# Two decoder layers on one core: gate and up weights resident, keys in two buffers, the first LayerNorm transposed on TensorE

## The chip, the cores and the metric

The kernel runs on one core of one Trainium2 chip. The metric is device time in microseconds (us) of one execution. Engines: PE is TensorE's matmul, PEld its weight load, DVE is VectorE, ACT is ScalarE, POOL is GpSimd, SP is SyncE, which issues all the transfers here.

## What is computed

Two layers, each a sliding-window attention block and a gated feed-forward block with residuals, over 2048 tokens of width 512 (bf16). Both layers use the same weights.

```python
def _A_ref(x, wqkv, wo):                 # H = 32 heads of 16, window W = 256
    qkv = (x @ wqkv).reshape(B, S, 3, H, Dh).transpose(2, 0, 3, 1, 4)
    q, k, v = qkv[0], qkv[1], qkv[2]
    scores = jnp.einsum("bhqd,bhkd->bhqk", q, k) * (Dh ** -0.5)
    mask = (idx[:, None] - idx[None, :] >= 0) & (idx[:, None] - idx[None, :] < W)
    scores = jnp.where(mask[None, None], scores, -1e9)
    o = jnp.einsum("bhqk,bhkd->bhqd", softmax(scores), v)
    return o.transpose(0, 2, 1, 3).reshape(B, S, D) @ wo

def _B_ref(x, w_gate, w_up, w_down):     # F = 1792
    h = sigmoid(x @ w_gate) * (x @ w_up)
    return h @ w_down

x = A_x
x = x + _A_ref(layernorm(x), A_wqkv, A_wo)
x = x + _B_ref(layernorm(x), B_w_gate, B_w_up, B_w_down)
x = x + _A_ref(layernorm(x), A_wqkv, A_wo)
x = x + _B_ref(layernorm(x), B_w_gate, B_w_up, B_w_down)
```

## The kernel before

The 2048 tokens are 16 tiles of 128, in four groups of 512. A group of a layer has the number gi = 4 * layer + group. The residual stream x stays in SBUF (`xsb`).

**Slots.** `run` (L459) writes the order of all instructions out by hand. It walks 256 slots: 16 tiles a layer, eight slots a tile, four heads a slot. A slot issues the scores of four heads (L337) into four fixed PSUM banks (`Sps`) and the exponential of them (L341) into a ring. Every second slot multiplies the diagonal block of eight heads by a triangular mask (L348) and, on POOL, cuts the far block (L353). Six slots after its scores, half a tile's values are summed (L366), copied (L371), transposed on PE a slot later (L383), normalized (L391, L393), transposed back by a DMA (L397), and two slots after that the output projection (L419) adds to x (L421).

**Streams.** The projections and the feed-forward parts are streams of units, put between: a projection stream has 12 units of four 512-column matmuls (keys and queries of four column groups, L224, and values of four tiles, L240). A GLU stream has 14 gate units (L284, then a tanh on ACT, L287), 14 up units (L295, then a multiply on DVE, L297), and three down units per tile (L307, then an add into x, L310); the half-group streams have 256 columns a unit in place of 512. After the last slot the streams that are left run alone: the tail. The list `order` (L464) ranks the streams; `next_stream` (L446) takes the first that has units, whose LayerNorm tiles are ready and whose `free_slot` has come, and never a second GLU stream before the first is done. Units are popped as long as the planner's nanoseconds leave room:

```python
if st_ is None or used + st_.units[0][0] // 2 > T_SLOT:
    break
```

`used` has 370 ns for scores, 868 for values, 228 for the transposes, 864 for an output projection. `ensure` (L433) pops what a slot needs and what isn't done yet. Keys, queries and values of a group go to buffers kTp[gi % 3] and Vaug[gi % 3]; `gi_free_slot` (L429) lets a projection stream start only when its buffers are free: slot 0 for gi 0 to 2, then 58, 90, 122, 154 and 186.

**LayerNorm.** `ln_stats` (L147) on DVE and a power on POOL, `ln_apply` (L158) on DVE one slot later, `ln_move` (L166) transposes a tile by a DMA from SP into `xnT`, which has three buffers of a group each; a tile counts as ready LN_LAG = 2 slots later. A LayerNorm whose group finds no free xnT buffer is put off slot by slot (L188). Groups 1 to 3 of layer 0 follow in slots 0 to 10.

**Weights.** wqkv, wo and w_down stay in SBUF. Gate and up weights are loaded again in each GLU stream, in seven chunks of 256 columns, through three buffers (`load_chunk`, L267), each chunk by two DMAs that the gate unit issues on SP's queue (L278), where the transposes are issued too, in order.

Of the kernel before, what the change touches and what calls it, by code (L numbers as in the profile page):

```python
# [11 lines left out]
P = 128  # L12
# [20 lines left out]
T_SLOT = 2000  # L33
# [27 lines left out]
class Net:  # L61
# [3 lines left out]
    def __init__(self, ctx, tc, A_x, wqkv, wo, w_gate, w_up, w_down, out):  # L65
# [15 lines left out]
        self.wgup = pool("wgu", 3)  # L81
# [17 lines left out]
        self.maskq = big.tile([P, 8, P], BF16, name="maskq")  # L99
# [30 lines left out]
        self.chunk_w = {}  # L130
        self.chunk_next = 0
        self.states = {}

    def constants(self):
        nc = self.nc
        for i in range(3):
            ones = self.Vaug[i][:, :, 0:VS * H].rearrange("p t (h c) -> p t h c", c=VS)[:, :, :, 16:VS]
            nc.gpsimd.memset(ones, 1.0)
            nc.gpsimd.memset(self.Vaug[i][:, :, VS * H:VW], 0.0)
            if i == 0:  # L140
                nc.gpsimd.memset(self.maskq[:], 1.0)
                nc.gpsimd.affine_select(out=self.maskq[:], in_=self.maskq[:], compare_op=ALU.is_ge, fill=0.0,
                                        base=0, pattern=[[0, 8], [1, P]], channel_multiplier=-1)
# [57 lines left out]
    def proj_stream(self, L, tg):  # L201
        key = ("p", L, tg)
        gi = L * NTG + tg
        b = gi % 3
        s = Stream(key, self.gi_free_slot(gi))
        tiles = range(tg * NBG, (tg + 1) * NBG)
        s.needs = [(key, t) for t in tiles]
        for cq in range(NCQ):
            for which in (1, 0):
                s.add(KT * T_MM, ("kq"[which == 0], gi, cq), lambda which=which, cq=cq: self._qk(key, tg, b, which, cq))  # L210
        for tt in range(NBG):
            s.add(KT * T_MM, ("v", gi, tt), lambda tt=tt: self._v(key, tg, b, tt))
        if gi == 0:
            v0 = s.units.pop(8)
            s.units.insert(4, v0)
        return s

    def _qk(self, key, tg, b, which, cq):
# [3 lines left out]
        c0 = which * D + cq * P  # L222
# [24 lines left out]
    def glu_stream(self, L, t0, n):
# [19 lines left out]
    def load_chunk(self):  # L267
        i = self.chunk_next
        self.chunk_next += 1
        f0 = (i % (FC // 2)) * 2 * P  # L270
        w = self.wgup.tile([P, KT, 2, 2 * P], BF16, name="wgu")
        self.nc.sync.dma_start(out=w[:, :, 0, :], in_=self.wg_src[:, :, f0:f0 + 2 * P])
        self.nc.sync.dma_start(out=w[:, :, 1, :], in_=self.wu_src[:, :, f0:f0 + 2 * P])
        self.chunk_w[i] = w

    def _gate(self, key, i, fc, c0, w):
# [41 lines left out]
    def scores(self, L, t, g):  # L318
# [13 lines left out]
        kTp = self.kTp[(L * NTG + t // NBG) % 3]  # L332
# [126 lines left out]
    def run(self):  # L459
        nc = self.nc  # L460
        self.slot = 0
        self.chunks = 0
        self.streams = []
        order = [("p", 0, 0), ("p", 0, 1), ("p", 0, 2), ("p", 0, 3), ("g", 0, 0, 2), ("g", 0, 2, 2), ("p", 1, 0),  # L464
                 ("g", 0, 4, 4), ("p", 1, 1), ("g", 0, 8, 4), ("p", 1, 2), ("g", 0, 12, 4), ("p", 1, 3),
                 ("g", 1, 0, 4), ("g", 1, 4, 4), ("g", 1, 8, 4), ("g", 1, 12, 2), ("g", 1, 14, 2)]
        for o in order:
            self.streams.append(self.proj_stream(*o[1:]) if o[0] == "p" else self.glu_stream(*o[1:]))
        k0 = ("p", 0, 0)
        for t in range(NBG):  # L470
# [13 lines left out]
        for t in range(NBG, 2 * NBG):  # L484
            self.at((t - NBG) // 2, 0, lambda t=t: self._ln_rest(("p", 0, 1), t))
        for t in range(2 * NBG, NT):
            self.at(t - 6, 0, lambda t=t: self.ln_later(("p", 0, t // NBG), t))
        self.at(12, 0, lambda: nc.vector.tensor_scalar(out=self.wd[:], in0=self.wd[:], scalar1=0.5, scalar2=None,
# [90 lines left out]
```

## Time and profile before

| | us |
|---|---|
| median of three runs | 680.45 |
| the fastest of them | 676.07 |
| the profiled execution | 677.35 |
| its span, first to last instruction | 675.6 |

The profiled execution is 1.75 us longer than its span. In the views, "busy" of PE counts matmuls that overlap in its pipeline. A figure after "<-" in brackets is idle time of that engine just before the instruction, and what ended it. PEclk is the clock granted to TensorE, as a share of full speed.

### The profile page before, as it was taken

To read this page: it belongs to the slowest core of one execution; us is meant where nothing else is said; L and a number is where in the kernel's file an instruction comes from. 1 tells how busy PE (TensorE), PEld (TensorE's weight loads), DVE (VectorE), ACT (ScalarE), POOL (GpSimd) and SP (SyncE) were. 2 spreads that over 40 slices of the span, in tenths; PEclk is the share of its full clock that TensorE was granted. 3 is DMA by queue.
4 is the path that set the end of the run, shared out by engine and by line. 5 is a ranking of instruction groups with operands and counts; after the bars stand their busy time and mean duration, and the time that the engine had idled before them with its cause. 6 is when DMAs were issued, how large, how long until landed. Compare 5 with 4: busy or idle time off the path is not lost.

```text
span 675.6 us, 17143 instructions
## 1 busy us (share of the span) xinstructions
PE 592.3 (88%) x7200; PEld 282.1 (42%) x7200; DVE 422.9 (63%) x851; ACT 459.1 (68%) x493; POOL 164.9 (24%) x191
## 2 busy tenths in 40 slices
PE   0689688686969999899998999999999998999697
PEld 0234354453423444444433444444444443445454
DVE  5497556658544656867588766866556656666322
ACT  0599666566876878766767897688868876752211
POOL 3352222223221222420023223322222222200000
PEclk9899899789868999999999999999999998999889
DMA  9621353352002420254113511243114522442553
GB/s 249 177 53 25 87 153 87 83 137 63 18 9 80 118 71 14 44 108 125 40 33 62 140 49 49 57 125 79 49 47 80 142 63 59 111 111 72 147 158 89
DMA packets 135629, 58.53 MB, mean 87 GB/s; under 512 B 55936, under 2 KB 135552, under 8 KB 135552
## 3 DMA queue, kind: packets, MB, share of 16 engines
q1 hardware_dynamic: 135552, 57.44, 33.4%
q8 instruction: 56, 0.92, 0.6%
q14 instruction: 21, 0.17, 0.1%
HBM read 42.73 MB, written 2.10 MB: 66 GB/s over the span
## 4 chain that ended last, share of the span: by engine, by line
PE 64%; ACT 12%; DVE 10%; DMA 9%; issue 2%; SPq 1%; POOL 1%; ACTq 0%; POOLq 0%; DVEq 0%
PE ups L295 14%; PE gps L284 13%; PE dps L307 10%; ACT PTring L341 9%; PE Sps L337 8%; PE proj_ps L224 7%; PE OTps L366 6%; PE OPps L419 3%; DMA wgu<-in_B_w_up_dram 3%; PE tps L383 2%; DVE xn L162 2%; DMA wgu<-in_B_w_gate_dram 2%; DVE ln_stats L152 2%; DVE PTring L348 2%; DMA xnT<-xn 2%
## 5 line engine op out<-in xcount | busy, mean ns | idle before, releaser
L341 ACT ACTIVATE PTring<-Sps 128x1536 bf16<-128x1536 f32 (+2 forms) x256 | 351.9, 1375 | 94.2 <-PE Sps L337 87.3
L353 POOL TENSOR_SCALAR_AFFINE_SELECT PTring<-PTring 128x1024 bf16<-128x1024 bf16 x112 | 124.4, 1113 | 182.5 <-ACT PTring L341 182.5
L284 PE MATMUL gps<-xnT,wgu 128*128 128x512 bf16 (+1 forms) x560 | 126.4, 351 | 20.7 <-DMA wgu<-in_B_w_gate_dram 14.9
L297 DVE SCALAR_TENSOR_TENSOR hT<-gth,ups 128x512 bf16<-128x512 bf16 (+1 forms) x140 | 81.0, 579 | 94.1 <-PE ups L295 71.5
L295 PE MATMUL ups<-xnT,wgu 128*128 128x512 bf16 (+1 forms) x560 | 126.5, 351 | 5.1 <-DMA wgu<-in_B_w_up_dram 1.7
L287 ACT ACTIVATE gth<-gps 128x512 bf16<-128x512 f32 (+1 forms) x140 | 71.3, 512 | 81.1 <-PE gps L284 76.2
L337 PE MATMUL Sps<-qT,kTp 32*128 32x128 bf16 (+2 forms) x1984 | 87.6, 248 | 25.6 <-ACT PTring L341 21.3
L155 POOL TENSOR_TENSOR ln_rs<-ln_rs,nhalf 128x1 f32<-128x1 f32 x64 | 38.3, 599 | 288.5 <-DVE ln_rs L154 283.6
L307 PE MATMUL dps<-wd,hT 128*128 128x512 bf16 x448 | 107.4, 380 | 0.0
L348 DVE TENSOR_TENSOR PTring<-PTring,maskq 128x1024 bf16<-128x1024 bf16 x128 | 98.8, 772 | 0.3 <-ACT PTring L341 0.2
L337 PEld LDWEIGHTS <-kTp 32*128 32x128 bf16 x1984 | 38.5, 93 | 128.5 <-issue 122.7
L224 PE MATMUL proj_ps<-xnT,wq 128*128 128x512 bf16 x256 | 66.9, 398 | 18.2 <-DMA xnT<-xn 17.2
L284 PEld LDWEIGHTS <-wgu 128*128 128x128 bf16 x560 | 51.9, 101 | 64.3 <-DMA wgu<-in_B_w_gate_dram 17.9
L295 PEld LDWEIGHTS <-wgu 128*128 128x128 bf16 x560 | 52.7, 102 | 49.1 <-issue 8.3
L371 DVE CAST OTs<-OTps 128x512 bf16<-128x512 f32 x64 | 44.1, 688 | 45.8 <-PE OTps L366 44.8
L307 PEld LDWEIGHTS <-hT 128*128 128x128 bf16 x448 | 40.3, 98 | 45.0 <-issue 2.5
L366 PE MATMUL OTps<-PTring,Vaug 128*32 128x128 bf16 x2880 | 53.2, 223 | 0.0
L162 DVE TENSOR_SCALAR xn<-xsb,ln_mv,ln_rs 128x512 bf16<-128x512 bf16 x64 | 47.5, 749 | 4.6 <-POOL ln_rs L155 3.8
L152 DVE BATCH_NORM_STATS2 ln_stats<-xsb 128x6 f32<-128x512 bf16 x64 | 44.3, 692 | 6.4 <-DMA xsb<-in_A_x_dram 4.8
L366 PEld LDWEIGHTS <-Vaug 128*32 128x32 bf16 x2880 | 41.8, 98 | 9.1 <-issue 5.7
L224 PEld LDWEIGHTS <-wq 128*128 128x128 bf16 x256 | 23.2, 101 | 44.9 <-DMA xnT<-xn 17.2
L310 DVE TENSOR_TENSOR xsb<-xsb,dps 128x512 bf16<-128x512 bf16 x32 | 21.9, 683 | 31.7 <-PE dps L307 31.4
(31 smaller groups left out, 304.4 us busy)
## 6 DMA issues: line engine op xcount, KB each, us to landing
wgu<-in_B_w_gate_dram SPq DMA_DIRECT2D x70, 256.0 KB, 3.2
wgu<-in_B_w_up_dram SPq DMA_DIRECT2D x70, 256.0 KB, 3.8
out_dram<-xsb SPq DMA_DIRECT2D x16, 128.0 KB, 1.7
wd<-in_B_w_down_dram SPq DMA_DIRECT2D x1, 1792.0 KB, 9.4
wq<-in_A_wqkv_dram SPq DMA_DIRECT2D x3, 512.0 KB, 6.0
xsb<-in_A_x_dram SPq DMA_DIRECT2D x3, 512.0 KB, 8.9
xnT<-xn SPq DMA_TRANSPOSE x64, 2.4
OnT<-On SPq DMA_TRANSPOSE x64, 2.3
```

The source lines that it names most:

```text
L162: nc.vector.tensor_scalar(out=xn[:], in0=self.xsb[:, t, :], scalar1=mv[:, 0:1], scalar2=rs[:, 1:2], op0=ALU.subtract, op1=ALU.mult)
L224: nc.tensor.matmul(pt[:], lhsT=self.wq[:, kt, c0:c0 + P], rhs=xnT[:, kt, :], start=(kt == 0), stop=(kt == KT - 1))
L284: nc.tensor.matmul(ps[:, 0:w], lhsT=wt[:, kt, 0, (fc % 2) * P:(fc % 2 + 1) * P], rhs=xnT[:, kt, c0:c0 + w], start=(kt == 0), stop=(kt == K ...
L287: nc.scalar.activation(out=self.th[:, 0:w], in_=ps[:, 0:w], func=AF.Tanh, scale=0.5)
L295: nc.tensor.matmul(ps[:, 0:w], lhsT=wt[:, kt, 1, (fc % 2) * P:(fc % 2 + 1) * P], rhs=xnT[:, kt, c0:c0 + w], start=(kt == 0), stop=(kt == K ...
L297: nc.vector.scalar_tensor_tensor(out=self.hT[:, fc, 0:w], in0=self.th[:, 0:w], scalar=1.0, in1=ps[:, 0:w], op0=ALU.add, op1=ALU.mult)
L307: nc.tensor.matmul(self.dps[:], lhsT=self.hT[:, fc, tt * P:(tt + 1) * P], rhs=self.wd[:, fc, :], start=(fc == 0), stop=(fc == FC - 1))
L337: nc.tensor.matmul(sps[:, m, i * P:(i + n) * P], lhsT=kTp[32 * m:32 * m + 32, cq, e, ko:ko + P], rhs=self.qT[32 * m:32 * m + 32, cq, (t + ...
L341: nc.scalar.activation(out=self.ring[:, h0:h0 + 7:2, p0:p0 + (nb - 1) * step + 1:step, :], in_=sps[:, :, 0:N].rearrange("p w (b c) -> p w ...
L348: nc.vector.tensor_tensor(out=r0, in0=r0, in1=self.maskq[:], op=ALU.mult)
L353: self.nc.gpsimd.affine_select(out=r2, in_=r2, compare_op=ALU.is_ge, fill=0.0, base=-1, pattern=[[0, 8], [-1, P]], channel_multiplier=1)
L366: nc.tensor.matmul(OT[32 * g:32 * g + 32, col, :], lhsT=Va[:, jj % NBG, VS * h:VS * h + 32], rhs=self.ring[:, h, ring_slot(jj, t - jj), :] ...
```

## The change

Gate and up weights get SBUF tiles of their own (`wg`, `wu`), loaded once; `load_chunk`, its pool and its 140 loads go. Room comes from kTp (two buffers in place of three), the mask (one 128-column block, read eight times, in place of eight blocks) and one xn buffer less. With two key buffers, keys of group gi may be made only from slot 32 (gi - 1) on, so the keys of later groups are streams of their own; values keep their three buffers and dates. A group's xnT is freed when all its units, the late keys too, are done. The four first tiles are transposed on PE and copied by ACT, and count as ready at once. Tiles 4 to 7 take their LayerNorm statistics in the slots in place of ahead of them. wo, then gate and up in quarters of 448 columns in turn, then w_down in two halves are issued on SP in slots 3, 5, ..., 23; the halving of w_down on DVE moves from slot 12 to 26. T_SLOT goes from 2000 to 1900.

```diff
-T_SLOT = 2000
+T_SLOT = 1900
...
-        self.ln_xn = pool("ln_xn", 4)
+        self.ln_xn = pool("ln_xn", 3)
...
+        self.wg = big.tile([P, KT, F], BF16, name="wg")
+        self.wu = big.tile([P, KT, F], BF16, name="wu")
...
-        self.kTp = [big.tile([P, NCQ, 2, TGW], BF16, name=f"kTp{i}") for i in range(3)]
+        self.kTp = [big.tile([P, NCQ, 2, TGW], BF16, name=f"kTp{i}") for i in range(2)]
...
-        self.maskq = big.tile([P, 8, P], BF16, name="maskq")
+        self.maskq = big.tile([P, 1, P], BF16, name="maskq")
...
-    def ln_move(self, key, t):
+    def ln_move(self, key, t, pe=False):
...
-        if LN_DMA:
+        if LN_DMA and not pe:
             nc.sync.dma_start_transpose(out=dst, in_=xn[:])
         else:
             pt = self.ps_d.tile([P, KT, P], BF16, name="ln_tp", tag="d")
             for c in range(KT):
                 nc.tensor.transpose(pt[:, c, :], xn[:, c * P:(c + 1) * P], self.ident[:])
-            nc.vector.tensor_copy(out=dst, in_=pt[:])
-        self.ready[key, t] = self.slot + (LN_LAG if LN_DMA else 1)
+            nc.scalar.copy(out=dst, in_=pt[:])
+        self.ready[key, t] = self.slot + (0 if pe else LN_LAG if LN_DMA else 1)
...
-    def proj_stream(self, L, tg):
+    def proj_stream(self, kinds, L, tg):
...
+        free = 0
+        if "k" in kinds and gi >= 2:
+            free = TGW // P * SLOTS_T * (gi - 1)
+        if "v" in kinds and gi >= 3:
+            free = max(free, (4 * (gi - 3) + 6) * SLOTS_T + 10)
+        s = Stream(key, free)
...
-        while self.chunk_next < min(i + 3 - (fc % 2 == 0), self.chunks):
-            self.load_chunk()
-        wt = self.chunk_w[i]
...
-            nc.tensor.matmul(ps[:, 0:w], lhsT=wt[:, kt, 0, (fc % 2) * P:(fc % 2 + 1) * P], rhs=xnT[:, kt, c0:c0 + w], start=(kt == 0),
+            nc.tensor.matmul(ps[:, 0:w], lhsT=self.wg[:, kt, fc * P:(fc + 1) * P], rhs=xnT[:, kt, c0:c0 + w], start=(kt == 0),
...
-        nc.vector.tensor_tensor(out=r0, in0=r0, in1=self.maskq[:], op=ALU.mult)
+        nc.vector.tensor_tensor(out=r0, in0=r0, in1=self.maskq[:].to_broadcast([P, 8, P]), op=ALU.mult)
...
-        order = [("p", 0, 0), ("p", 0, 1), ("p", 0, 2), ("p", 0, 3), ("g", 0, 0, 2), ("g", 0, 2, 2), ("p", 1, 0),
-                 ("g", 0, 4, 4), ("p", 1, 1), ("g", 0, 8, 4), ("p", 1, 2), ("g", 0, 12, 4), ("p", 1, 3),
+        order = [("kqv", 0, 0), ("kqv", 0, 1), ("qv", 0, 2), ("qv", 0, 3), ("g", 0, 0, 2), ("k", 0, 2), ("g", 0, 2, 2),
+                 ("qv", 1, 0), ("k", 0, 3), ("k", 1, 0), ("g", 0, 4, 4), ("qv", 1, 1), ("k", 1, 1), ("g", 0, 8, 4),
+                 ("qv", 1, 2), ("k", 1, 2), ("g", 0, 12, 4), ("qv", 1, 3), ("k", 1, 3),
                  ("g", 1, 0, 4), ("g", 1, 4, 4), ("g", 1, 8, 4), ("g", 1, 12, 2), ("g", 1, 14, 2)]
...
-        for t in range(NBG, 2 * NBG):
-            self.ln_stats(("p", 0, 1), t)
         self.constants()
-        nc.sync.dma_start(out=self.wot[:], in_=self.wo_src)
-        nc.sync.dma_start(out=self.wd[:], in_=self.wd_src)
...
+        loads = [load(self.wot[:], self.wo_src)]
+        for i in range(4):
+            h = slice(i * F // 4, (i + 1) * F // 4)
+            loads += [load(self.wg[:, :, h], self.wg_src[:, :, h]), load(self.wu[:, :, h], self.wu_src[:, :, h])]
+        loads += [load(self.wd[:, i * 7:i * 7 + 7, :], self.wd_src[:, i * 7:i * 7 + 7, :]) for i in range(2)]
+        for i, fn in enumerate(loads):
+            self.at(3 + 2 * i, 0, fn)
+        self.at(26, 0, lambda: nc.vector.tensor_scalar(out=self.wd[:], in0=self.wd[:], scalar1=0.5, scalar2=None,
```

## Rows read from the trace of the kernel before

**Rows 1.** Page, busy us (share of the span) and instructions of an engine:

```profile
PE 592.3 (88%) x7200; PEld 282.1 (42%) x7200; DVE 422.9 (63%) x851; ACT 459.1 (68%) x493; POOL 164.9 (24%) x191
```

**Rows 2.** Stages: us, busy us (instructions) by engine, PEclk, DMA share, GB/s:

```profile
17.20:77.50 60.30, 50.03 (x516) 21.54 (x516) 42.48 (x98) 51.99 (x60) 22.00 (x30) 0.97 0.31 72
77.50:205.00 127.50, 97.00 (x1362) 53.71 (x1363) 74.29 (x147) 85.55 (x89) 33.41 (x35) 0.85 0.33 85
...
336.00:617.00 281.00, 270.33 (x3414) 120.49 (x3413) 189.77 (x359) 211.94 (x208) 74.66 (x80) 0.99 0.31 77
617.00:675.60 58.60, 48.14 (x357) 30.60 (x354) 20.49 (x46) 11.22 (x29) 0.55 (x1) 0.94 0.46 129
```

**Rows 3.** PE's waits from 77 to 160 us: total us, times, longest:

```profile
PE gps L284 <- DMA wgu<-in_B_w_gate_dram: 8.6, 3, 4.4
PE gps L284 <- DMA xnT<-xn: 2.9, 1, 2.9
```

**Rows 4.** PE's waits from 617 to 676 us, the tail:

```profile
PE gps L284 <- DMA wgu<-in_B_w_gate_dram: 5.9, 3, 2.6
PE ups L295 <- DMA wgu<-in_B_w_up_dram: 1.0, 4, 0.3
```

**Rows 5.** Timeline of the start: start us, us, engine, line, operation [idle before]:

```profile
8.08 7.04 SPq L174 DMA_TRANSPOSE xnT<-xn  x4
8.43 0.41 DVE L162 TENSOR_SCALAR xn<-xsb,ln_mv,ln_rs 128x512 bf16<-128x512 bf16 x1 [0.44 <-POOL ln_rs L155]
...
17.23 3.57 PE L224 MATMUL proj_ps<-xnT,wq 128*128 128x512 bf16 x8 [17.23 <-DMA xnT<-xn]
...
19.13 0.59 ACT L230 CAST kt<-proj_ps 128x512 bf16<-128x512 f32 x1 [17.05 <-PE proj_ps L224]
```

**Rows 6.** Timeline, the exponentials of slots 0, 1 and 2:

```profile
21.86 1.45 ACT L341 ACTIVATE PTring<-Sps 128x1536 bf16<-128x1536 f32 x1 [0.44 <-PE Sps L337]
...
23.76 1.45 ACT L341 ACTIVATE PTring<-Sps 128x1536 bf16<-128x1536 f32 x1 [0.44 <-PE Sps L337]
...
27.88 1.45 ACT L341 ACTIVATE PTring<-Sps 128x1536 bf16<-128x1536 f32 x1 [0.45 <-PE Sps L337]
```

**Rows 7.** Timeline at slot 24, where the first gates begin:

```profile
76.13 1.19 SPq L174 DMA_TRANSPOSE xnT<-xn  x1
...
78.67 0.57 SPq L272 DMA_DIRECT2D wgu<-in_B_w_gate_dram  x1
...
81.84 1.03 PE L284 MATMUL gps<-xnT,wgu 128*128 128x256 bf16 x4 [4.36 <-DMA wgu<-in_B_w_gate_dram]
```

**Rows 8.** Timeline of slots 69 and 70, which have no stream units:

```profile
195.56 0.51 PE L337 MATMUL Sps<-qT,kTp 32*128 32x384 bf16 x4 [1.69 <-ACT PTring L341]
...
196.17 1.45 ACT L341 ACTIVATE PTring<-Sps 128x1536 bf16<-128x1536 f32 x1 [0.67 <-PE Sps L337]
...
198.42 1.45 ACT L341 ACTIVATE PTring<-Sps 128x1536 bf16<-128x1536 f32 x1 [0.80 <-PE Sps L337]
```

**Rows 9.** Instruction groups by shape: busy us, mean ns | idle before, releasers:

```profile
L348 DVE TENSOR_TENSOR PTring<-PTring,maskq 128x1024 bf16<-128x1024 bf16 x128 | 98.8, 772 | 0.3 <-ACT PTring L341 0.2
...
L393 DVE TENSOR_TENSOR On<-tps,Rt 128x256 bf16<-128x256 bf16 x64 | 27.2, 424 | 2.3 <-DVE Rt L391 0.2
```

**Rows 10.** Page, DMA issues: KB each (or none), median us from issue to landing:

```profile
wd<-in_B_w_down_dram SPq DMA_DIRECT2D x1, 1792.0 KB, 9.4
...
xnT<-xn SPq DMA_TRANSPOSE x64, 2.4
```

**Rows 11.** The wqkv loads: ns of an issue, first and last start; us to landing:

```profile
L109 SPq DMA_DIRECT2D wq<-in_A_wqkv_dram x3: 433/507/508, 2.7 to 3.7; - x3
...
DMA to landing us min/median/max: 5.0/6.0/7.0
```

**Rows 12.** Timeline, up matmuls just after the first gates' wait and later:

```profile
82.66 1.06 PE L295 MATMUL ups<-xnT,wgu 128*128 128x256 bf16 x4
...
86.16 0.60 PE L295 MATMUL ups<-xnT,wgu 128*128 128x256 bf16 x4
```

More of the change, by code (lines that the diff above doesn't have):

```diff
@@ L129, in __init__ @@
         self.xnT = {}
-        self.chunk_w = {}
-        self.chunk_next = 0
+        self.left = {}
         self.states = {}
@@ L197, in _ln_rest @@
             self.at(1, KT * T_TR, lambda: self.ln_move(key, t))
-    def proj_stream(self, L, tg):
+    def proj_stream(self, kinds, L, tg):
         key = ("p", L, tg)
         gi = L * NTG + tg
[L204 to L207, printed above, removed]
-        for cq in range(NCQ):
[L209 to L212, printed above, removed]
+        free = 0
[4 more added lines that the diff above has]
+        s = Stream(key, free)
+        s.needs = [(key, t) for t in range(tg * NBG, (tg + 1) * NBG)]
+        self.left[key] = self.left.get(key, 0)
+        for cq in range(NCQ):
+            for k in kinds:
+                if k in "kq":
+                    self.left[key] += 1
+                    s.add(KT * T_MM, (k, gi, cq), lambda k=k, cq=cq: self._qk(key, tg, gi % 2, k, cq))
+        if "v" in kinds:
+            for tt in range(NBG):
+                self.left[key] += 1
+                s.add(KT * T_MM, ("v", gi, tt), lambda tt=tt: self._v(key, tg, gi % 3, tt))
         if gi == 0:
@@ L216, in proj_stream, with used_up, _qk @@
         return s
-    def _qk(self, key, tg, b, which, cq):
+    def used_up(self, key):
+        self.left[key] -= 1
+        if self.left[key] == 0:
+            del self.xnT[key]
+    def _qk(self, key, tg, b, k, cq):
         nc = self.nc
@@ L221, in _qk @@
         pt = self.ps_d.tile([P, TGW], F32, name="proj_ps", tag="d")
-        c0 = which * D + cq * P
+        c0 = (k == "k") * D + cq * P
         for kt in range(KT):
@@ L225, in _qk @@
                              start=(kt == 0), stop=(kt == KT - 1))
-        if which == 0:
+        self.used_up(key)
+        if k == "q":
             nc.scalar.copy(out=self.qT[:, cq, tg * TGW:(tg + 1) * TGW], in_=pt[:])
@@ L243, in _v @@
         nc.scalar.copy(out=vdst, in_=pt[:].rearrange("p (h e) -> p h e", e=16))
-        if tt == NBG - 1:
-            del self.xnT[key]
+        self.used_up(key)
     def glu_stream(self, L, t0, n):
@@ L254, in glu_stream @@
         c0 = (t0 % NBG) * P
-        base = self.chunks
-        self.chunks += FC // 2
         last = (t0 + n) % NBG == 0
         for fc in range(FC):
-            s.add(KT * (w / 2.4 + 3), None, lambda fc=fc: self._gate(key, base + fc // 2, fc, c0, w))
-            s.add(KT * (w / 2.4 + 3), None, lambda fc=fc: self._up(key, base + fc // 2, fc, c0, w, last))
+            s.add(KT * (w / 2.4 + 3), None, lambda fc=fc: self._gate(key, fc, c0, w))
+            s.add(KT * (w / 2.4 + 3), None, lambda fc=fc: self._up(key, fc, c0, w, last))
         cuts = [0, 5, 10, FC]
@@ L265, in glu_stream, with _gate @@
         return s
[L267 to L276, printed above, removed]
+    def _gate(self, key, fc, c0, w):
         nc = self.nc
-        while self.chunk_next < min(i + 3 - (fc % 2 == 0), self.chunks):
-            self.load_chunk()
-        wt = self.chunk_w[i]
         xnT = self.xnT[key]
@@ L287, in _gate, with _up @@
         nc.scalar.activation(out=self.th[:, 0:w], in_=ps[:, 0:w], func=AF.Tanh, scale=0.5)
-    def _up(self, key, i, fc, c0, w, last):
+    def _up(self, key, fc, c0, w, last):
         nc = self.nc
-        wt = self.chunk_w[i]
         xnT = self.xnT[key]
@@ L294, in _up @@
         for kt in range(KT):
-            nc.tensor.matmul(ps[:, 0:w], lhsT=wt[:, kt, 1, (fc % 2) * P:(fc % 2 + 1) * P], rhs=xnT[:, kt, c0:c0 + w], start=(kt == 0),
+            nc.tensor.matmul(ps[:, 0:w], lhsT=self.wu[:, kt, fc * P:(fc + 1) * P], rhs=xnT[:, kt, c0:c0 + w], start=(kt == 0),
                              stop=(kt == KT - 1))
@@ L473, in run, with load @@
                 self.ln_apply(k0, t - 1)
-                self.ln_move(k0, t - 1)
+                self.ln_move(k0, t - 1, True)
         self.ln_apply(k0, NBG - 1)
-        self.ln_move(k0, NBG - 1)
-        for t in range(NBG, 2 * NBG):
-            self.ln_stats(("p", 0, 1), t)
+        self.ln_move(k0, NBG - 1, True)
         self.constants()
-        nc.sync.dma_start(out=self.wot[:], in_=self.wo_src)
-        nc.sync.dma_start(out=self.wd[:], in_=self.wd_src)
         for tag in (("k", 0, 0), ("q", 0, 0)):
             self.ensure(tag)
[L484 to L488, printed above, removed]
+        for t in range(NBG, NT):
+            self.at((t - NBG) // 2 if t < 2 * NBG else t - 6, 0, lambda t=t: self.ln_later(("p", 0, t // NBG), t))
+        def load(dst, src):
+            return lambda: nc.sync.dma_start(out=dst, in_=src)
+        loads = [load(self.wot[:], self.wo_src)]
[6 more added lines that the diff above has]
+        self.at(26, 0, lambda: nc.vector.tensor_scalar(out=self.wd[:], in0=self.wd[:], scalar1=0.5, scalar2=None,
                                                        op0=ALU.mult))
```

10 lines of the change are left out of this document (3 added, 7 removed).

## Prediction

> **What bounds the kernel now.** I read the busy times first. TensorE works 592.3 of 675.6 us [rows 1], so the time is TensorE's work plus some 83 us in which it has nothing to do, plus what it loses where the clock is granted at half. The table by stage says where these are [rows 2]. In the long middle (336 to 617 us) TensorE is busy 270.33 of 281.00 us at a clock of 0.99: nothing but less work shortens that stage. In the stage from 17.2 to 77.5 us (the first three projections) it is busy 50.03 of 60.30, from 77.5 to 205 us only 97.00 of 127.50 at a clock of 0.85, and in the tail, after the last exponential, 48.14 of 58.60. The 17.2 us before the first matmul make up the rest. So a change can win at the start, in the first third and in the tail, and what it does to the middle is only a shift.
>
> The waits name what ends these idle times. Between 77 and 160 us TensorE waits 8.6 us in three waits for the gate weights' transfer and 2.9 us once for a transposed LayerNorm tile [rows 3]; in the tail 5.9 us in three waits for gate weights and 1.0 for up weights [rows 4]. The timeline shows why the first is long: the load is issued by the first gate unit itself, behind a transpose on SP's queue, at 78.67 us; the gates start at 81.84 after 4.36 us idle [rows 7]. At the start, the four DMA transposes take SP from 8.08 to 15.12 us although the last normalized tile is written at 8.84, and the first projection starts at 17.23 [rows 5].
>
> Below TensorE's work lies a slot's own loop: scores, exponential, scores, since the next scores need the PSUM that the exponential reads. Slot 0, with nothing but that loop, lasts 23.76 - 21.86 = 1.9 us [rows 6]: the floor. In a stretch of the first third without stream work the scores alone take 0.51 us, TensorE waits 1.69 for the exponential, and a slot lasts 198.42 - 196.17 = 2.25 us [rows 8]. Such slots cost nearly as much as full ones (the 599.8 us from 17.2 to the tail [rows 2] over 256 slots are 2.3) and carry nothing: work put into them is almost free.
>
> **The change, part by part.**
>
> *First LayerNorm on TensorE.* Removed: four DMA transposes. Added: 16 transposes and four copies on ScalarE, which idles until 19.13 [rows 5]. The last tile is ready at 8.84. Four 256-column matmuls took 1.06 us at low clock [rows 12]; for four transposes of 128 columns I take 0.65. The copy is 512 columns out of PSUM, like the 0.59 us kt copy [rows 5]. 8.84 + 0.65 + 0.6 + 0.15 for two handovers = 10.25 us. The key weights are issued at 2.7 and the three parts land 5.0 to 7.0 us after their issue [rows 11]: 9.7 at worst for the first, not later than the tile. Saved: 17.23 - 10.25 = 7.0; if the query part, issued in the middle, were the last to come (about 10.2), the same; bounds 5.5 to 7.3.
>
> *Early slots.* A DMA-moved tile counts as ready two slots later; a TensorE-moved one at once. So the first stream may fill slots 0 and 1, two units each, and the keys of column group 1 are there when slot 2 wants them; before, slot 1 lasted 27.88 - 23.76 = 4.1 us on that chain [rows 6], 2.2 over the floor, and there is one more slot of the kind. Up to 4 us saved. One unit is four 512-column matmuls, 0.87 us. Before slot 24 the streams then have 32 units in place of 36 (keys of group 2 come later), 4 x 0.87 = 3.5 us less, so they run dry at about slot 17 in place of 22. From there slots run at the floor: 1.9 if TensorE stays warm, 2.25 if not, against about 2.2 before. I take 2 us saved for the whole of it: bounds 0 and 5.
> The long slot [rows 8] decides how much of this is kept. [...]
>
> *Resident gate and up weights.* Removed: 140 loads of 256 KB through three buffers, and all waits for them. In layer 0 8.6 us [rows 3]; but what is late next at 77.48? The transpose of tile 1 is issued at 76.13 and takes 2.4 us to land, 78.55 [rows 7, 10]: 1.1 us of the first wait stays. So 7.5 saved. [...] In the middle stage 1 us. [...] Bounds for all of this: 13 (other waits appear behind them) to 22.
>
> *Bulk loads.* 5.9 MB in 11 loads at slots 3 to 23, with their issues in SP's queue among transposes. Before, the 1792 KB of down weights took 9.4 us to land [rows 10]; at that pace a 448 KB piece takes 2.4 us, about one slot, and one is issued every second slot. A transpose behind one lands up to 2.4 us later than its 2.4; the LayerNorm tiles of this time are used several slots later, an output projection two slots (4.4 us) after its transpose: covered, unless a transpose also waits. The halving of the down weights (a VectorE pass of about 2 us) moves from slot 12 to slot 26, beside the first gates, where up results wait for VectorE: I take 1 us lost, bounds 0 and 5.
>
> *Keys in two buffers.* The keys of group n can be made only from slot 32(n-1), and are wanted at 32n: no burst. Group 2's four units come after the first half-tile GLU, about slots 37 to 40, where TensorE has little: the 2.9 us wait for a transposed tile lies there [rows 3]. They cost almost nothing and push the second half-tile GLU behind its tile's landing: 1.5 saved, bounds -1.5 (units delay the tile too) and 2.9. Later key units move by six slots within full slots: nothing. Three xnT buffers are held longer by the late keys; walking the slots, only layer 1's first tiles wait (to about slot 41), and they are not used before slot 90.
>
> *T_SLOT 1900.* A full slot has used 370, 598 (with transposes) or about 1236 ns before streams. A 865 ns unit is taken while used + 432 is within T_SLOT: 598 + 865 = 1463 still passes 1467, so gates, ups and projections stay at 13 per 8 slots. Down units (1080) drop from 11 to 10 per 8 slots, some 7 slots' worth or 10 us of matmuls moved into the tail over the kernel. Where slots are bound by TensorE they shorten by as much; where the floor binds they don't. Bounds 0 and 10 lost; as 270 of 281 us are busy [rows 2], I take 2.
>
> *Small mask, read eight times.* VectorE's mask multiply takes 772 ns for 1024 elements. The nearest row with a broadcast source is the 256-element On, 424 ns [rows 9], which repeats single elements and reads PSUM; at its pace the mask would take 1.7 us, 128 x 0.92 = 118 us more on VectorE. Here whole rows of 128 repeat, so I take 0, nearest to the old mask.
> [...]
>
> Sum: 7.0 + 2 + 7.5 + 1.7 + 1 + 8.6 + 1.5 - 1 - 2 = 26.3 less, 675.6 - 26.3 = 649.3 of span, and 1.75 around it as before (677.35 - 675.6): 651.0. The median shown, 680.45, is 3 us above the profiled run, which I count as spread.
>
> **Rivals.**
> *The next wait takes the place of the weights'.* In layer 0 each GLU also waits for its LayerNorm tile (1.1 at slot 24, 2.9 later), and slots are counted, not timed: faster slots bring the tile later in slots. Then layer 0 gives back its 7.5 + 1.7 + 1.5: 661.7. For it: the row at 76.13; against: the second and third weight waits had no tile behind them.
> *The floor eats the smaller slots.* Everything as forecast, but the 10 us of down matmuls moved land in the tail with no shorter slots: 659. For it: slots near 1.9; against: a middle 96% busy.
> *More is won.* Early slots win 5 us in place of 2, the weights 22 in place of 18.8, the tile wait goes whole (1.4), floor and bulk loads cost nothing (3): 10.6 more, 640.4. For it: a clock of 0.85 over 127.5 us leaves much to regain [rows 2]; against: emptied slots run cold.
> [...]
>
> **How the numbers follow.** Forecast 0.50 (644 to 657), next wait 0.17, floor 0.12, more won 0.14, slower 0.04, others 0.03 either way. Range 637 to 666, which leaves the mask, part of the best case and mishaps out. About 2% is what a measurement of this kernel can tell from no change: 667 against the median. Forecast, more won, most of the floor and three quarters of the next-wait case lie under it: faster 0.84, same 0.11, slower 0.05.
>
> **What would show it.** First projection near 10.3 us and released by ScalarE's copy or the key weights; no DMA wait for gate or up weights anywhere; slots 17 to 23 without streams; key units about slots 38 and 64; the mask still near 0.77 us; the tail with TensorE busy all but its last 4 us. It is wrong if the mask rises over 1 us, if bulk loads delay transposes so that output projections wait, or if TensorE's share in the middle falls.

## The result, and the profile after

The changed kernel takes 641.74 us (median of 641.18 to 642.07) against 679.69 before: a ratio of 0.946, interval 0.942 to 0.950. The forecast was 651.0, range 637 to 666. The profiled execution spans 640.0 us, 35.6 less than before, where the sum of the prediction had 26.3. One of the four times of the kernel before was 3052 us; the ratio leaves it out, and the median of the other three is 678.93.

Busy times of the changed kernel (the page's first part):

```profile
PE 580.9 (91%) x7216; PEld 281.8 (44%) x7216; DVE 423.5 (66%) x851; ACT 460.4 (72%) x497; POOL 166.4 (26%) x191
```

This line against [rows 1] divides the gain. Idle time of TensorE fell from 83.3 to 59.1 us, by 24.2. Its busy time fell from 592.3 to 580.9, by 11.4, although it has 16 transposes more to do (2.4 us): the same matmuls ran faster. In the prediction 22.9 us of the sum were idle time and 3.4 us clock. So in the sum the idle time came out as worked out, and the clock was taken at a quarter to a third of what it gave.

The stages, cut at the same slots as [rows 2] (slot 24, just after slot 72, slot 129, the last exponential); columns as there, the third row being the stage that [rows 2] leaves out:

```profile
10.30:70.30 60.00, 47.91 (x500) 20.66 (x499) 41.35 (x99) 49.77 (x56) 22.03 (x27) 0.91 0.57 139
70.30:182.30 112.00, 92.77 (x1377) 52.35 (x1378) 77.20 (x158) 86.70 (x93) 34.19 (x35) 0.95 0.14 31
182.30:309.30 127.00, 122.68 (x1542) 54.57 (x1541) 83.65 (x161) 96.11 (x106) 28.32 (x31) 0.98 0.10 20
309.30:583.90 274.60, 262.47 (x3384) 117.96 (x3382) 191.74 (x364) 212.34 (x209) 76.32 (x80) 1.00 0.11 24
583.90:640.00 56.10, 52.66 (x404) 34.79 (x401) 23.79 (x50) 11.84 (x30) 0.55 (x1) 1.00 0.09 27
```

The second row is the heart of it: 112.0 us in place of 127.5, with TensorE idle 19 in place of 30 us, and a granted clock of 0.95 in place of 0.85. The first row is 60.0 us, as long as before (60.3), with four units less in it and a lower clock (0.91 against 0.97). The tail is 2.5 us shorter and holds more matmuls. By stage the idle time agrees less well than in the sum: the second row loses 11.3 us of it, where the terms for it (7.5 + 1.5 - 1) had 8.0, and the first row has 1.8 us more, where the early slots were to save 2. That the sums agree is in part luck.

At the start, timeline of the changed kernel:

```profile
8.46 0.52 DVE L162 TENSOR_SCALAR xn<-xsb,ln_mv,ln_rs 128x512 bf16<-128x512 bf16 x1 [0.44 <-POOL ln_rs L155]
9.04 0.61 PE L178 MATMUL ln_tp<-ident,xn 128*128 128x128 bf16 x4 [0.35 <-DVE xn L162]
9.68 0.58 ACT L179 COPY xnT<-ln_tp 128x512 bf16<-128x512 bf16 x1 [0.37 <-PE ln_tp L178]
10.32 3.40 PE L237 MATMUL proj_ps<-xnT,wq 128*128 128x512 bf16 x8 [0.67 <-ACT xnT L179]
```

The chain is the one of the prediction, and the projection starts at 10.32 in place of 17.23 [rows 5].

### The profile page after: what moved, and what is told of

It reads as the page before. It is cut to its first block, busy times and chain, and to the rows that moved or that the text cites. A ratio compares the mean times of both kernels' runs of the same rounds, so it can differ in the third digit from the quotient of the medians.

```text
span 640.0 us, 16976 instructions
## 1 busy us (share of the span) xinstructions
PE 580.9 (91%) x7216; PEld 281.8 (44%) x7216; DVE 423.5 (66%) x851; ACT 460.4 (72%) x497; POOL 166.4 (26%) x191
## 3 DMA queue, kind: packets, MB, share of 16 engines
q1 hardware_dynamic: 63696, 23.87, 15.9%
## 4 chain that ended last, share of the span: by engine, by line
PE 58%; ACT 16%; DVE 14%; issue 6%; DMA 4%; POOL 1%; ACTq 0%; POOLq 0%; DVEq 0%
PE ups L293 13%; PE gps L283 13%; ACT PTring L339 13%; PE dps L305 9%; PE Sps L335 7%; PE OTps L364 5%; PE OPps L417 4%; DMA OnT<-On 3%; DVE ln_stats L152 3%; DVE xn L162 3%; DVE PTring L346 2%; PE proj_ps L237 2%; PE v_ps L254 2%; PE tps L381 2%; DVE OTs L369 1%
## 5 line engine op out<-in xcount | busy, mean ns | idle before, releaser
L351 POOL TENSOR_SCALAR_AFFINE_SELECT PTring<-PTring 128x1024 bf16<-128x1024 bf16 x112 | 127.3, 1138 | 168.3 <-ACT PTring L339 166.8
L295 DVE SCALAR_TENSOR_TENSOR hT<-gth,ups 128x512 bf16<-128x512 bf16 (+1 forms) x140 | 81.1, 579 | 74.7 <-PE ups L293 63.8
L283 PE MATMUL gps<-xnT,wg 128*128 128x512 bf16 (+1 forms) x560 | 122.7, 342 | 4.5 <-DMA xnT<-xn 2.1
L293 PE MATMUL ups<-xnT,wu 128*128 128x512 bf16 (+1 forms) x560 | 121.6, 340 | 3.4 <-DVE hT L295 2.3
L346 DVE TENSOR_TENSOR PTring<-PTring,maskq 128x1024 bf16<-128x1024 bf16 x128 | 97.2, 760 | 2.4 <-ACT PTring L339 2.4
L283 PEld LDWEIGHTS <-wg 128*128 128x128 bf16 x560 | 51.4, 99 | 44.3 <-issue 7.6
L293 PEld LDWEIGHTS <-wu 128*128 128x128 bf16 x560 | 51.2, 98 | 41.9 <-issue 8.8
L237 PE MATMUL proj_ps<-xnT,wq 128*128 128x512 bf16 x256 | 63.7, 387 | 1.9 <-DMA xnT<-xn 1.1
L419 DVE TENSOR_TENSOR xsb<-xsb,OPps 128x512 bf16<-128x512 bf16 x32 | 21.9, 686 | 46.9 <-PE OPps L417 46.9
L417 PE MATMUL OPps<-wot,OnT 128*128 128x512 bf16 x128 | 36.0, 397 | 3.7 <-DMA OnT<-On 3.6
```

The source lines that it names most:

```text
L237: nc.tensor.matmul(pt[:], lhsT=self.wq[:, kt, c0:c0 + P], rhs=xnT[:, kt, :], start=(kt == 0), stop=(kt == KT - 1))
L283: nc.tensor.matmul(ps[:, 0:w], lhsT=self.wg[:, kt, fc * P:(fc + 1) * P], rhs=xnT[:, kt, c0:c0 + w], start=(kt == 0), stop=(kt == KT - 1))
L293: nc.tensor.matmul(ps[:, 0:w], lhsT=self.wu[:, kt, fc * P:(fc + 1) * P], rhs=xnT[:, kt, c0:c0 + w], start=(kt == 0), stop=(kt == KT - 1))
L295: nc.vector.scalar_tensor_tensor(out=self.hT[:, fc, 0:w], in0=self.th[:, 0:w], scalar=1.0, in1=ps[:, 0:w], op0=ALU.add, op1=ALU.mult)
L346: nc.vector.tensor_tensor(out=r0, in0=r0, in1=self.maskq[:].to_broadcast([P, 8, P]), op=ALU.mult)
L351: self.nc.gpsimd.affine_select(out=r2, in_=r2, compare_op=ALU.is_ge, fill=0.0, base=-1, pattern=[[0, 8], [-1, P]], channel_multiplier=1)
```

## The experiments

A time is a median with the ratio to the kernel before and its 95% interval. The table has the length in us of the stages of each profiled execution, cut at the exponentials of slots 0, 24, 72, 128 and 255, and the mean granted clock of TensorE. The changed kernel alone was timed once, beside a kernel before of 679.69; the experiments were timed in three later groups, beside a kernel before of 678.82 (e1, e2, e3, e9), 677.04 (e4 to e7) and 678.07 us (e8, e10 to e12). So a difference of about 2 us to the changed kernel lies within what the groups differ by.

| kernel | to slot 0 | 0 to 24 | 24 to 72 | 72 to 128 | 128 to 255 | tail | clock |
|---|---|---|---|---|---|---|---|
| before | 21.9 | 55.7 | 125.1 | 130.3 | 283.9 | 58.8 | 0.957 |
| LayerNorm on TensorE alone (e3) | 16.6 | 53.8 | 127.1 | 129.8 | 285.0 | 61.4 | 0.949 |
| key streams alone (e9) | 21.8 | 55.6 | 121.3 | 127.2 | 281.5 | 55.3 | 0.971 |
| one key group alone (e10) | 21.7 | 55.6 | 121.8 | 130.2 | 282.0 | 58.6 | 0.969 |
| before, thin slots filled (e6) | 22.0 | 58.0 | 123.6 | 125.8 | 281.0 | 58.2 | 0.985 |
| changed | 14.8 | 55.6 | 109.6 | 126.3 | 277.5 | 56.1 | 0.979 |
| changed, weights streamed (e2) | 14.3 | 55.0 | 124.2 | 126.0 | 277.1 | 63.6 | 0.972 |
| changed, T_SLOT 2000 (e1) | 15.2 | 56.6 | 114.3 | 127.6 | 281.0 | 47.8 | 0.971 |
| changed, loads first (e4) | 15.0 | 63.8 | 111.2 | 125.1 | 277.9 | 56.1 | 0.968 |
| changed, ready later (e12) | 14.3 | 58.6 | 109.8 | 126.0 | 279.2 | 56.4 | 0.976 |
| changed, thin slots filled (e5) | 15.0 | 56.0 | 108.0 | 123.3 | 277.8 | 56.8 | 0.999 |
| changed, queries early (e7) | 15.3 | 56.5 | 109.5 | 128.3 | 277.3 | 51.9 | 0.979 |
| all three additions (e8) | 14.4 | 57.3 | 106.7 | 123.7 | 278.5 | 52.1 | 0.997 |

### One part undone or done alone: e1, e2, e3, e9

*Weights streamed again (e2).* The chunk loads come back, and the eight bulk loads of gate and up weights go; all else stays.

```diff
-        self.wg = big.tile([P, KT, F], BF16, name="wg")
-        self.wu = big.tile([P, KT, F], BF16, name="wu")
+        self.wgup = pool("wgu", 3)
...
+        while self.chunk_next < min(i + 3 - (fc % 2 == 0), self.chunks):
+            self.load_chunk()
```

> The changed kernel with gate and up weights streamed through three buffers as before; all else is kept (keys in two buffers, first LayerNorm on TensorE, T_SLOT 1900). Theory A: the waits come back, 8.6 + 1.1 + 6.9 us, and with them stretches at the lower clock, some 6 to 9 us: 660 to 667 us, with a mean clock near 0.965. Rival B (order and budget made the surplus): only the idle times come back, 653 to 658 us.

Measured: 661.9 us, 0.975 (0.970 to 0.980). The weights are worth 20.2 us, inside theory A's range. By the page of this kernel 15.9 us of it are idle time of TensorE (75.0 against 59.1) and 4.3 busy time:

```profile
PE 585.2 (89%) x7216; PEld 281.1 (43%) x7216; DVE 424.6 (64%) x851; ACT 461.2 (70%) x497; POOL 165.6 (25%) x191
```

TensorE's waits in this kernel from slot 24 to 72, and in its tail (total us, times, longest):

```profile
PE gps L298 <- DMA wgu<-in_B_w_gate_dram: 13.4, 4, 7.5
PE ups L309 <- DMA wgu<-in_B_w_up_dram: 0.7, 2, 0.4
```

```profile
PE gps L298 <- DMA wgu<-in_B_w_gate_dram: 2.9, 4, 1.6
PE ups L309 <- DMA wgu<-in_B_w_up_dram: 2.2, 5, 1.2
```

By the table 14.6 us of it lie between slots 24 and 72 and 7.5 in the tail, nothing elsewhere. The wait of 7.5 us is longer than any of before [rows 3], so in this order streaming costs more in layer 0 than it did.

*Key streams alone (e9).* The kernel before with two key buffers and the new list of streams; weights streamed, T_SLOT 2000, LayerNorm by DMA.

```diff
-        self.kTp = [... for i in range(3)]
+        self.kTp = [... for i in range(2)]
...
-        order = [("p", 0, 0), ("p", 0, 1), ("p", 0, 2), ("p", 0, 3), ("g", 0, 0, 2), ...
+        order = [("kqv", 0, 0), ("kqv", 0, 1), ("qv", 0, 2), ("qv", 0, 3), ("g", 0, 0, 2), ("k", 0, 2), ...
```

> The kernel before with keys in two buffers and their own unit streams in the new order, weights still streamed, T_SLOT 2000, LayerNorm by DMA. Theory A: it only moves units: 677 to 682 us. Rival B (units put into the thin slots of layer 0 are the surplus): 669 to 673 us.

Measured: 664.54 us, 0.979 (0.973 to 0.985): 14.3 us less, past even what rival B expected. Theory A, by which the keys only move, has fallen. The page and two stages of this kernel:

```profile
PE 583.3 (88%) x7200; PEld 278.7 (42%) x7200; DVE 420.1 (63%) x851; ACT 458.5 (69%) x493; POOL 169.1 (26%) x191
```

```profile
77.40:201.00 123.60, 95.94 (x1378) 52.95 (x1379) 74.14 (x155) 87.16 (x93) 34.12 (x35) 0.90 0.35 88
...
607.50:662.70 55.20, 46.40 (x363) 29.54 (x360) 21.21 (x47) 11.26 (x29) 0.55 (x1) 1.00 0.55 139
```

The span is 12.9 us shorter; TensorE's busy time, with the same 7200 matmuls, is 9.0 us shorter than in [rows 1], and only 3.9 us are idle time. So in the profiled execution the key streams pay mostly in the clock: 0.90 against 0.85 in the first third, 1.00 against 0.94 in the tail [rows 2].

*LayerNorm on TensorE alone (e3).* The kernel before, with

```diff
-                self.ln_move(k0, t - 1)
+                self.ln_move(k0, t - 1, True)
```

> The kernel before with the first four LayerNorm tiles transposed on TensorE and nothing else. Theory A: first projection near 10.3 us, and the 7 us stay to the end: 671 to 674 us. Rival (the earlier start is given back in the first slots, where tiles 4 to 7 and the weight loads are waited for): 676 to 680 us.

Measured: 672.82 us, 0.992 (0.989 to 0.994), 6.0 us less, as theory A had it. The table shows 5.3 us to slot 0 and 1.9 between slots 0 and 24, and some given back later. Its profiled run is the slowest of its ten (675.38 us) and has the lowest clock (0.949); their mean is 0.957, as in the kernel before, so the lower clock of that profile is no effect of the edit.

*T_SLOT back at 2000 (e1).*

```diff
-T_SLOT = 1900
+T_SLOT = 2000
```

> The changed kernel with T_SLOT back at 2000. Theory A (the surplus over the forecast is TensorE's clock, which the weight waits had been lowering; the slot budget only shifts work between slots and tail): 640 to 644 us, the tail about 8 us shorter and the slots as much longer. Rival B (the smaller budget spreads work into the thin slots of layer 0 and that is the surplus): 648 to 652 us.

Measured: 643.58 us, 0.948 (0.943 to 0.953), 1.8 us over the changed kernel, with overlapping intervals. The tail is 8.3 us shorter, near what the unit count of the prediction had (10 us), and the slots are longer by 10.5 in all. The budget is no source of the surplus.

### Is it the clock? e6, e5

Matmuls that nobody reads, in slots with room and no stream unit; nothing is left out of the computation.

```diff
+            while st_ is None and 4 <= s < 120 and used + KT * T_MM // 2 <= T_SLOT:
+                used += self.keep_warm()
...
+    def keep_warm(self):
+        pt = self.ps_d.tile([P, D], F32, name="warm", tag="d")
+        for kt in range(KT):
+            self.nc.tensor.matmul(pt[:], lhsT=self.wq[:, kt, 0:P], rhs=self.wq[:, kt, 0:D], start=(kt == 0), stop=(kt == KT - 1))
+        return KT * T_MM
```

> The kernel before with matmuls of no use (four 512-column matmuls of resident weights into a spare PSUM tile, read by nobody) in those slots of 4 to 119 that have room and no stream unit; nothing is left out. Theory C (a thin slot costs as much as a full one because TensorE falls to its lower clock, and the work after it runs slow too): half-clock time falls from 59.6 us to 25 to 35 and the time to 668 to 674 us, though TensorE does more. Rival (thin slots cost their floor and the added matmuls only get in the way): 679 to 684 us.

> The changed kernel with the same matmuls of no use in its thin slots. Theory C: half-clock time falls from 27.8 us to under 12 and the time to 635 to 640 us. Rival: 641 to 646 us.

Measured: the kernel before so filled takes 671.16 us, 0.990 (0.985 to 0.995), 5.9 less than the kernel before beside it; the changed one 637.93, 0.941 (0.938 to 0.945), 3.8 less than without. Their clocks, and the stage of e6 that [rows 2] shows as the second:

```profile
core 0: 668.7 us, clock 0.985
```

```profile
77.50:205.00 127.50, 111.39 (x1475) 58.86 (x1472) 75.37 (x151) 86.60 (x90) 34.63 (x36) 0.96 0.34 86
```

```profile
core 0: 637.0 us, clock 0.999
```

100 more matmuls (380 ns each, overlapping, 24.4 us of TensorE's busy time) made the kernel before faster, and 92 the changed one; both times are as theory C had them. The clock's records of the kernel before and of the changed one hold two levels, 1.00 and 0.50 (1.00 from 86 to 88 us before, 0.50 from 195.5 to 198.5). By such records, which reach a little past the span, time at the lower level fell from 59.6 to 22.0 us before (expected: 25 to 35; mean clock 0.957 to 0.985) and from 27.8 to 3.3 after (0.979 to 0.999); per us at the lower level 0.16 us are won in both, not 0.5. TensorE's waits for gate weights stay (14.9 us in all before, 14.4 in e6), those for transposed tiles fall by 2.5 us.

The table shows where the gain lies. Between slots 24 and 72, where 88 of the 100 matmuls stand, e6 is only 1.5 us shorter. Between slots 72 and 128, with the same 1538 matmuls and none of the added ones, it is 4.5 us shorter. Before, and e6:

```profile
202.70:333.00 130.30, 124.55 (x1538) 54.82 (x1539) 87.12 (x171) 95.56 (x106) 29.21 (x32) 0.96 0.31 77
```

```profile
203.70:329.50 125.80, 120.82 (x1538) 53.95 (x1539) 86.82 (x170) 95.52 (x105) 29.05 (x32) 1.00 0.32 79
```

There 3.7 us of the 4.5 are busy time of the same matmuls, so this part is the clock's. In e5 the same slots are 3.0 us shorter than in the changed kernel. So the second half of theory C is shown: the work behind thin slots runs slow, and where TensorE is busy nearly all the time a us at the lower level (9.2 us in these slots before, none in e6) costs about half a us. The first half is not: the stage of the thin slots stays about as long at a clock of 0.96 as at 0.85, with the added matmuls in it. There the exponential's loop most likely hides a slow TensorE.

### Which key units pay? e10

```diff
-        order = [("p", 0, 0), ("p", 0, 1), ("p", 0, 2), ("p", 0, 3), ("g", 0, 0, 2), ("g", 0, 2, 2), ...
+        order = [("kqv", 0, 0), ("kqv", 0, 1), ("qv", 0, 2), ("kqv", 0, 3), ("g", 0, 0, 2), ("k", 0, 2), ("g", 0, 2, 2), ...
```

> The kernel before, three key buffers and all dates kept, with nothing moved but the four key units of layer 0's third group: from its projection stream (about slots 16 to 23) to just behind the first half-group GLU (about slots 37 to 40). If the gain of the keys' own streams is this one filling of thin slots: 667 to 672 us, the transposed-tile wait near slot 40 gone. If it is spread over all the later key units too: 674 to 678 us.

Measured: 673.85 us, 0.994 (0.992 to 0.997), 4.2 us less, between the two expectations and nearer the second. By the table it has the whole gain of e9 between slots 24 and 72 (121.8 against 121.3) and none between 72 and 128 (130.2 against 127.2) or in the tail (58.6 against 55.3). So filling the thin slots 37 to 40 is about 4 us; the other 10 of e9 belong, by subtraction, to the later key units, whose moves the prediction put at nothing. They are not all clock. The time lost to the lower level is about one minus the mean granted clock, times the time: over all runs some 29 us in the kernel before (0.957), 24.6 in e10 (0.964) and 19.6 in e9 (0.971). By this estimate e10's gain is all clock, and e9's is some 10 us of clock and 4 of idle time, which agrees with its page. Part of the 3.1 us that e9 wins between slots 72 and 128 is work that goes to the stage behind (the keys of group 5 may not start before slot 128): it is one unit of four matmuls, 0.9 us. The stage behind takes it, gives five down matmuls to the tail, and is 2.4 us shorter all the same. Why the tail's weight waits are then all near 1 us or under, I can't trace to a single cause. That stays open.

### The loads and the early units: e4, e12

```diff
-            self.at(3 + 2 * i, 0, fn)
+            fn()
```

> The changed kernel with all eleven bulk loads issued in a row ahead of slot 0, not spread over slots 3 to 23. If the spreading matters: the transposes of tiles 4 to 7 stand behind 5.9 MB on SP's queue and in the transfer engines, and the second projection stream starts late, 647 to 655 us. If the first slots cover it: 640 to 643 us.

Measured: 650.99 us, 0.961 (0.958 to 0.964), 9.2 over the changed kernel; 8.2 us of it lie between slots 0 and 24 and 1.6 between 24 and 72. SP's queue at the start, and TensorE's wait:

```profile
20.32 3.17 SPq L477 DMA_DIRECT2D wd<-in_B_w_down_dram  x2
23.61 19.40 SPq L174 DMA_TRANSPOSE xnT<-xn  x8
```

```profile
PE proj_ps L237 <- DMA xnT<-xn: 9.8, 1, 9.8
```

The first of the tiles' transposes is issued at 23.61 us, behind eleven loads, in place of 19.75, and TensorE stands 9.8 us for them. Spreading is worth 9 us; without it the resident weights would have lost nearly half of what they bring.

```diff
-        self.ready[key, t] = self.slot + (0 if pe else LN_LAG if LN_DMA else 1)
+        self.ready[key, t] = self.slot + (LN_LAG if LN_DMA else 1)
```

> The changed kernel with the tiles transposed on TensorE counted as ready two slots later, like those moved by DMA, so that the first stream may not fill slots 0 and 1. If the early units are worth what the forecast gave (2 us): 643 to 645 us. If what they win is lost again in the emptied slots ahead of slot 24, which cost as much as full ones: 641 to 642.5 us.

Measured: 644.27 us, 0.951 (0.946 to 0.955), 2.5 us over the changed kernel: the early units are worth about what the forecast gave. The table has 3.0 us of it between slots 0 and 24.

### A faster version: e7, e8, e11

*Queries early (e7).* The queries of layer 0's last group need no free buffer, and those of layer 1's first group none after slot 32.

```diff
-... ("qv", 0, 2), ("qv", 0, 3), ("g", 0, 0, 2), ("k", 0, 2), ("g", 0, 2, 2), ("qv", 1, 0), ("k", 0, 3), ("k", 1, 0), ...
+... ("qv", 0, 2), ("q", 0, 3), ("v", 0, 3), ("g", 0, 0, 2), ("k", 0, 2), ("g", 0, 2, 2), ("q", 1, 0), ("k", 0, 3), ("v", 1, 0), ("k", 1, 0), ...
```

> The changed kernel with the queries of two groups taken out of their streams: those of layer 0's last group go into slots 17 to 24 (before: 58 on), those of layer 1's first group to about slot 60 (before: 90 on). Theory C (units put into thin slots are free and keep the clock up): 634 to 639 us. Rival (thin slots behind take the place of those filled): 640 to 643 us.

Measured: 639.59 us, 0.944 (0.940 to 0.948), 2.2 less than the changed kernel, at the border of the two expectations and no proof of either. In its table row the tail is 4.2 us shorter, which are the units put forward; some 3 us of that are lost between slots 0 and 128.

*All three (e8)*: e7, the filled thin slots, and the down weights loaded in slots 13 and 15 and halved in slot 19.

```diff
+        loads[5:5] = [load(self.wd[:, i * 7:i * 7 + 7, :], self.wd_src[:, i * 7:i * 7 + 7, :]) for i in range(2)]
...
-        self.at(26, 0, lambda: nc.vector.tensor_scalar(out=self.wd[:], ...
+        self.at(19, 0, lambda: nc.vector.tensor_scalar(out=self.wd[:], ...
```

> The changed kernel with the queries of two groups in thin slots (as in e7), the matmuls of no use in slots that stay thin (as in e5), and the down weights loaded in slots 13 and 15 and halved in slot 19, ahead of the gates. If the three gains add up (2 + 4 + 1): 633 to 636 us. If they draw on the same idle time: 636 to 639 us.

Measured: 634.8 us (634.44 to 635.78), 0.937 (0.933 to 0.942), 6.9 less than the changed kernel, in the range that was expected if the three add up. Two of them gave 2.2 and 3.8 us alone; the third, the earlier down weights, was not run alone. With e11 it is the fastest of both kernels and their variants.

*Warm start (e11)*: e8 with nine matmuls of no use between 3 us and the first projection.

```diff
+            if t > 0:
+                self.warm_start(6 if t == 1 else 1)
...
+            self.nc.tensor.matmul(pt[:], lhsT=self.ident[:], rhs=self.xsb[:, 0, :], start=True, stop=True)
```

> As e8, and in addition nine 512-column matmuls of no use between 3 us and the first projection, between the LayerNorm transposes. If the clock is raised by any matmul activity, the first eight projection matmuls take 1.9 us in place of 3.4 and the time is 1.5 to 2.5 us under e8. If not, e8's time or 0.5 us over it.

Measured: 634.75 us, of four runs two at 632.4 and 632.9 and two at 636.6 and 636.9. The profiled one is of the slower pair:

```profile
10.39 3.57 PE L237 MATMUL proj_ps<-xnT,wq 128*128 128x512 bf16 x8 [0.67 <-ACT xnT L179]
```

Its first eight projection matmuls are as slow as in the kernel before [rows 5]; in e8's profile, without the nine matmuls, they take 2.97 us, in the changed kernel's 3.40. The mean clock is 0.997 in all four runs and does not tell the pairs apart; the faster pair has no trace. Inconclusive: in the mean nothing, and more spread.

## Why the prediction was right, and where it was not

*The start* (7.0) was sized right: 10.32 us against 10.25 in the working.

*The early slots* (2) came about as they were worked out, e3 having 1.9 there and e12 2.5 to 3.0. But the changed kernel's stage from slot 0 to 24 is as long as before. By the table slot 24 comes at 77.6 us before and at 70.4 both in e3 and in the changed kernel: the start and the early slots together gave 7.2 us, not 9. What divides the changed kernel's 14.8 + 55.6 from e3's 16.6 + 53.8 was not run part by part; one difference is the statistics of tiles 4 to 7, which now stand in the slots. Another is the bulk loads. TensorE's waits of the changed kernel between 15 and 72 us, and the start of SP's queue there, are

```profile
PE Sps L335 <- ACT PTring L339: 7.6, 9, 2.0
PE OPps L417 <- DMA OnT<-On: 1.5, 1, 1.5
PE proj_ps L237 <- DMA xnT<-xn: 1.1, 1, 1.1
```

```profile
19.75 5.91 SPq L174 DMA_TRANSPOSE xnT<-xn  x4
25.71 0.57 SPq L477 DMA_DIRECT2D wot<-in_A_wo_dram  x1
```

The wait for an output transpose, 1.5 us at 47 us, stands among loads; the prediction called it covered. The wait of 1.1 us for a tile is not the loads': it ends at 27.06 us, the transposes of tiles 4 to 7 are issued ahead of the first load, and e2 has the same wait (0.8 us). And e2, without eight of the eleven loads, is only 0.6 us shorter in this stage. So with the halving of the down weights (1.1, below) the *bulk loads* cost between 1.7 and 2.6 us, not 1: inside their bounds, a term mis-sized. A 448 KB load took 4.1 us to land, not the 2.4 of the working:

```profile
wg<-in_B_w_gate_dram SPq DMA_DIRECT2D x4, 448.0 KB, 4.1
```

The emptied slots save next to nothing: the eight slots from 16 to 24 take 16.7 us with almost no stream unit (2.1 a slot, between the 1.9 and the 2.25 of the working), against 17.1 before, at a clock that falls to the lower level:

```profile
56.00:70.00 14.00, 7.92 (x124) 4.10 (x123) 6.57 (x12) 10.17 (x8) 4.39 (x5) 0.63 0.50 147
```

TensorE is busy 7.92 of these 14 us, at a granted clock of 0.63, which is 0.50 from 60 to 66 us and 1.00 again from 80 to 90, among the gates.

*The weights* (18.8 with their clock): 20.2 in e2, 15.9 of them idle time and 4.3 busy time, where the sum had 15.4 and 3.4. This step was right in its mechanism and in its size. Its two terms of 1.7 us for the clock behind the weight waits (one of them in the tail's 8.6, beside 6.9 of waits [rows 4]) were the author's estimate, and no run shows them. What the runs showed in their place is the 4.3 us of busy time and, in the kernel before, a granted clock of 0.50 from 81.84 to 84 us, behind the first wait, and of 1.00 from 86 to 88. Nor does a run show the 1 us for the middle stage: slots 128 to 255 take 277.1 us in e2 and 277.5 in the changed kernel. What the prediction named as late next is what the trace of the changed kernel shows at slot 24:

```profile
69.70 1.19 SPq L174 DMA_TRANSPOSE xnT<-xn  x1
...
72.21 1.01 PE L283 MATMUL gps<-xnT,wg 128*128 128x256 bf16 x4 [1.96 <-issue]
...
78.61 2.02 DVE L486 TENSOR_SCALAR wd<-wd 128x7168 bf16<-128x7168 bf16 x1
...
81.03 0.60 PE L293 MATMUL ups<-xnT,wu 128*128 128x256 bf16 x4 [1.06 <-ACT gth L286]
...
181.94 1.86 PE L283 MATMUL gps<-xnT,wg 128*128 128x512 bf16 x4 [2.07 <-DMA xnT<-xn]
```

The gates wait 1.96 us for something that the profile doesn't name, and 69.70 + 2.4 = 72.1 is when the tile should land: most likely the first rival's mechanism, at this place nearly twice the 1.1 us allowed for it. It shows once more, by name, at 181.94 us, where the third GLU waits 2.07 us for its tile (1.67 in the kernel before). The second GLU's wait of 2.9 us [rows 3] is gone. The halving of w_down keeps VectorE 2.02 us, and an up unit waits 1.06 there, the 1 us of the prediction. The profile puts this wait on ScalarE's tanh; in e8, with the halving seven slots earlier, it is gone. In the tail no wait for a transfer is left. The last one, 1.1 us for an output transpose, ends at 580.21 us, just ahead of it:

```profile
PE OPps L417 <- DMA OnT<-On: 1.1, 1, 1.1
```

*The keys in two buffers* (1.5) is the step that failed: "Later key units move by six slots within full slots: nothing". Alone they gave 14.3 us (e9), 4 in the slots that the prediction named (e10) and 10 elsewhere. Only 3.9 us are idle time that the units found; by the records of the clock TensorE spent 20 us less at its lower level, and its busy time fell by 9.0. The prediction counted clock only right behind weight waits, 3.4 us, and left the clock of 0.85 over the first third to a rival. The parts overlap, since e2, e9, e3 and e1 add up to 42 us and the change gave 37 to 38: most likely because a stretch at the lower clock that one part ends can't be ended by another.

*The smaller slots* (2 lost): the count of down units was about right (10 us; 8.3 left the tail in e1), the loss was not there: 1.8 us won, within the noise. The rival of the floor has no support.

*The mask* cost nothing. VectorE's row after is

```profile
L346 DVE TENSOR_TENSOR PTring<-PTring,maskq 128x1024 bf16<-128x1024 bf16 x128 | 97.2, 760 | 2.4 <-ACT PTring L339 2.4
```

760 ns against 772 [rows 9], so the slower case (0.04) did not come: here a row read eight times runs at the pace of the full mask.

The time lies near the case "more is won" (640). The reason named there, that a low clock leaves much to regain, is the right one, but it had no price: the terms that make up the 640 did not come (early slots 5, weights 22, bulk loads at nothing). That the case names the time to 2 us is luck, and so is part of the range that held. Two of the prediction's own signs of being wrong show, both small: an output projection waits 1.5 us behind loads, and TensorE's share of the middle is 95.6% after 96.2%. And one reading was off, without weight in the sum: the median of 680.45 is one of three times that include the 3052 us.

## What to carry to other kernels

Compare TensorE's busy time before and after a change that leaves its matmuls alone: what it lost there was clock here (9.0 us in e9, at a mean clock of 0.971 in place of 0.957), and it is to be priced for every stretch with a low granted clock, above all for the full slots behind it (4.5 us between slots 72 and 128 in e6, 3.7 of them busy time of the same matmuls), and not only behind the wait that is removed. Thin slots are a good place for units that are free to move (4.2 us for four key units in e10), and here even matmuls of no use paid there (5.9 us in e6, 3.8 in e5). Bulk loads that share a queue with small urgent transfers should be spread between them, which was worth 9 us here.

## What was not expected of the hardware

Adding 100 matmuls that nobody reads shortened a kernel whose TensorE was 88% busy by 5.9 us (0.985 to 0.995). Nine such matmuls before the first projection left its first eight matmuls at 3.57 us in the run with a profile (2.97 without the nine, in e8), and split four runs into two pairs 4 us apart.
